# Norm sums by pairs, an earlier second batch, and four rest rows together in the head of a linear-attention and two-MLP kernel

## The chip, the cores and the metric

One core of one Trainium2 chip. The metric is the device time of one execution in microseconds. Before the change three runs took 1415.94, 1416.15 and 1416.86; the median is 1416.15.

## The reference

```python
kv  = einsum('bhsd,bhse->bhde', k, v)        # batch 8, heads 8, seq 576, head_dim 64
o   = einsum('bhsd,bhde->bhse', q, kv)
o   = o / sqrt(mean(o * o, axis=-1) + 1e-6) * g_norm
x   = o.transpose(0, 2, 1, 3).reshape(4608, 512)
h   = x @ w_in                               # 512 x 2048
x2  = (h * cos(h)) @ w_out                   # 2048 x 512
out = ((x2 @ w1) * (x2 @ w2)) @ w3 @ w_out2  # d_ff 1024
```

All arithmetic is float32 or finer; the weights arrive as 64-bit floats.

## The kernel before, in words

The order of every engine's instructions is written out by hand (`manual_schedule`): an engine runs its instructions in the order in which the Python code issues them, and waits at one whose operands are not there. So is the order of the DMA queue on SyncE (SP).

**Units, pairs, tiles.** A batch has two units (halves of 288 rows) and four pairs of heads. Units 0 and 1 are the first batch, 2 and 3 the second. The tokens are cut into tiles of 512 rows (TB); the products with `w_in` go in steps. Steps 0 to 7 are tile 0 with the eight first 128-column chunks of `w_in`, steps 8 to 15 tile 1 with the same chunks, and so on. A step is `emit_h`: twelve TensorE matmuls of 512 columns, because both `x` and `w_in` are held as a high and a low half (float32r) and three products of the halves are summed for each of four row blocks. In steps 0 to 8 the products that need the halves that come last stand last (L1065).

**What a step needs and leaves.** `w_in[m]` is made from chunk m: ScalarE and VectorE turn 64-bit words into float32 by five instructions (L157 on ScalarE, then L158, L159, L162, L167 on VectorE; `begin()` issues the first, `two()` the next two), and `put` splits the result: the high half on ScalarE (L123), the low half (L125) on VectorE for chunks 0 and 6 and on GpSimd for the others. Behind a step, ScalarE rounds (`rounded`, L654), VectorE reduces the angle (`reduced`, L657), ScalarE takes the sine (`sine`, L662) and VectorE multiplies by h (`gelu`, L666); this last one releases the step's bank. In the later loop (`phases`) the same four are L1942, L1943, L1912 and L1913.

**Norms.** For each pair and unit, ScalarE squares the outputs (`emit_square`) and keeps a scaled copy (`emit_keep`). `emit_sums` sums the squares over the head dimension on TensorE: 128 x 32 weights that pick a row, 96 columns at a time (T3), three matmuls for each unit. Their results land in 32 output partitions given by the pair (`place(p)`). Nine VectorE instructions (`norms`) take the inverse root of all at once. Then a spread brings each row back to 128 partitions: matmuls of 32 x 128 weights (`emit_row`, L502), one row group of 32 partitions for each pair, and VectorE multiplies the kept outputs by them (`emit_scale`, L519). `split_x` makes the high half of x (ScalarE, L1025) and the low half (VectorE or GpSimd, L1026).

A bank of PSUM holds 512 columns, but two units of a pair have 576. So the first spread covers 512 of them, and the remaining 64 are spread one pair at a time between the later steps (`rest_of`, one lone matmul). The second spread covers 480; the remaining 96 of unit 3 are done at the top of steps 8, 9, 10 and 11 (`left_row`), and their scaling in the middle of these (`left_scale`). All of these rests use the bank acc3, which step 6 also uses.

**Order around the change.** `first_batch` runs the first batch's kv sums, outputs, squares, sums, norms and spread, the second batch's kv sums, step 0, and the second batch's outputs of pair 0. `first_steps` runs steps 1 to 8 with the second batch in them: pair n's squares and sums in step n, its outputs a step earlier; then its norms, the spread and the low halves of tile 1. `phases` follows: at step n it issues step n + 1 on TensorE, the events of later batches (step 10's is the first, kv sums of the third batch, in the bank acc2 of step 8), and the four instructions of step n. Loads of the third batch's k and v wait in SP's queue for the buffers ("stage") in which the rounded values of steps 6 and 7 lie, its second pair of query loads for a buffer of the spread's weights.

Of the kernel before, what the change touches and what calls it, by code (L numbers as in the profile page):

```python
# [7 lines left out]
F32 = mybir.dt.float32  # L8
# [26 lines left out]
def kernel(  # L35
# [182 lines left out]
    def put_w_in(m):  # L218
        def put(f):
            t = wi_tile(m, f"w_in{m}")  # L220
            split(t.rearrange("p i k f -> p i (k f)"), f, nc.vector if m in (0, 6) else nc.gpsimd)
            w_in[m] = t
        return put

# [257 lines left out]
            o_sb[u] = ap.tile([P, NPAIR, HALF], F32, tag="osb", bufs=3, name=f"o_{u}")  # L482
        nc.scalar.activation(o_sb[u][:, p, :], o_ps.pop((u, p)), AF.Identity, scale=gneg)

    def place(p):
        return slice(32 * p, 32 * p + 32)

    def emit_sums(p, us, sums):
        for u in us:
            for k in range(NT3):  # L490
                i = 2 * (NT3 * (u % NHALF) + k)
                nc.tensor.matmul(
                    sums[place(p), 0:T3], picks["sums"][:, IN_ALL - i:IN_ALL - i + 32],
                    squares[u, p][:, T3 * k:T3 * k + T3], start=i == 0, stop=True,
                    skip_group_check=True,
                )
        for u in us:
            squares.pop((u, p))

    def emit_row(u, p, k, y, ps, c, start=True, part=slice(0, T3)):  # L500
        at = place(p)
# [5 lines left out]
    def emit_rows(us, width, banks, y):  # L507
        c = 0
        for u in us:
            for k in range(NT3):  # L510
                w = min(T3, width - c)
                for p in range(NPAIR):
                    if w > 0:
                        emit_row(u, p, k, y, banks[p], c, c == 0, slice(0, w))
                c += w

    def emit_scale(u, p, ps, c, s=slice(0, HALF)):
        o = o_sb[u][:, p, s]
        nc.vector.tensor_tensor(o, o, ps[:, c:c + s.stop - s.start], ALU.mult)  # L519

    def emit_scales(us, p, ps, width):
        emit_scale(us[0], p, ps, 0)
        emit_scale(us[1], p, ps, HALF, slice(0, width - HALF))

    def norms(sums, y):

# [4 lines left out]
    def first_batch(y, ones, g_row):  # L531

        sums = ps_h.tile([P, 512], F32, tag="h", name="ms_first")
        idle = ps_h.tile([P, 512], F32, tag="h", name="idle")
        units, seconds = range(NHALF), range(NHALF, 2 * NHALF)

        def begin():
            c = chunks[state["conv"]]
            state["conv"] += 1
            made = c.convert()  # L540
            next(made)
            return made
# [12 lines left out]
        emit_kv(0, 0, lambda: busy(2))  # L555
        copy_kv(0)
        g_ps = ps_a.tile([P, 512], F32, tag="pa", name="g_ps")
        nc.tensor.matmul(
            g_ps[:, 0:1], g_row, ones[:, 0:1],
            start=True, stop=True,  # L560
        )
        busy(2)
        for p in range(NPAIR):
            for u in units:
                emit_whole(u, p, ps_acc.tile(
                    [P, 512], F32, tag=f"acc{(2 * p + u) % 4}", name=f"out_{u}_{p}"
                )[:, 0:HALF])
            for u in units:
                emit_square(u, p)
            if p == 2:  # L570
                first = begin()
            if p + 1 < NPAIR:
                emit_kv(0, p + 1)
                copy_kv(p + 1)
            else:
                busy(4)
                rest_of(first)
                put(1)
            if p == 0:
                nc.scalar.activation(gneg, g_ps[:, 0:1], AF.Copy, scale=-1.0)  # L580
            emit_sums(p, units, sums)
            for u in units:
                emit_keep(u, p)
        list(norms(sums, y))
        emit_kv(1, 0)
        copy_kv(0)
        second = begin()
        rest_of(second, 2)
        busy(4)
        emit_kv(1, 1)  # L590
        copy_kv(1)
        banks = [
            ps_acc.tile([P, 512], F32, tag=f"acc{p}", name=f"spread1_{p}") for p in range(NPAIR)
        ]
        emit_rows(units, TB, banks, y)
        later = ps_h.tile([P, 512], F32, tag="h", name="kv_later0")
        emit_kv(1, 2, ps=later[:, 0:D])
        emit_kv(1, 3)
        for p in range(2):
            emit_scales(units, p, banks[p], TB)  # L600
            split_x(0, p, lows=nc.gpsimd)
        h = emit_h_parts(0)
        next(h)
        next(h)
        for p in range(2, NPAIR):
            emit_scales(units, p, banks[p], TB)
        for p in range(2, NPAIR):
            split_x(0, p)
        copy_kv(2)
        copy_kv(3)  # L610
        next(h)
        next(h)
        for v in seconds:
            out_bank(v, 0)
        next(h, None)
        third = begin()
        rest_of(second, 2)
        put(1)
        emit_h(1)
        rest_of(third, 2)  # L620
        return third

    def out_bank(v, p):
        emit_whole(v, p, two_banks(v, p, f"out_{v}_{p}")[:, 0:HALF])
# [6 lines left out]
    def first_steps(y_first, y, made):  # L631

        units = range(NHALF, 2 * NHALF)
        far = units[-1]
# [38 lines left out]
        def more():  # L673
            prefetch(min(state["put"] + 8, n_first))

        WIDE = HALF + 2 * T3
        cut = TB - HALF

        def rest_of(p):
            ps = ps_acc.tile([P, 512], F32, tag="acc3", name=f"spread1_rest{p}")  # L680
            emit_row(1, p, NT3 - 1, y_first, ps, 0, part=slice(cut - 2 * T3, T3))
            return ps

        more()
        for n in range(NPAIR):
            if n:
                gelu(n - 1)
                rest = rest_of(n - 1)
                emit_h(n + 1)
            rounded(n)  # L690
            reduced(n)
            if n:
                keep(n - 1)
            for v in units:
                emit_square(v, n)
            two(made)
            if n:
                emit_scale(1, n - 1, rest, 0, slice(cut, HALF))
            sine(n)
            new = begin()  # L700
            put(1)
            more()
            two(new)
            made = new
            emit_sums(n, units, sums)
            if n + 1 < NPAIR:
                for v in units:
                    out_bank(v, n + 1)
        n = NPAIR
        gelu(n - 1)  # L710
        rest = rest_of(n - 1)
        emit_h(n + 1)
        rounded(n)
        reduced(n)
        keep(n - 1)
        two(made)
        emit_scale(1, n - 1, rest, 0, slice(cut, HALF))
        sine(n)
        new = begin()
        norm = norms(sums, y)  # L720
        next(norm)
        put(1)
        more()
        emit_h(n + 2, "acc3")
        next(norm, None)
        spread = [
# [13 lines left out]
        split_x(1, slice(0, KD), (NHALF - 1,), nc.gpsimd)  # L740
        for p in range(NPAIR):
            emit_scales(units, p, spread[p], WIDE)
            if p < 2:
                split_x(1, p, units, nc.gpsimd)
        reduced(n + 1)
        split_x(1, 2, units)
        split_x(1, 3, units)
        emit_h(HM)
        sine(n + 1)
        gelu(n + 1)  # L750
# [2 lines left out]
        rounded(n + 3)  # L753
        new = begin()
        gelu(n + 2)
        reduced(n + 3)
        sine(n + 3)
        two(new)
        gelu(n + 3)
        two(new)  # L760
        spare.append(chunks[HM].tag)
        put(1)

        left = {}

        def left_row(p):
            left[p] = ps_acc.tile([P, 512], F32, tag="acc3", name=f"spread2_rest{p}")
            emit_row(far, p, NT3 - 1, y, left[p], 0)

        def left_scale(p):  # L770
            emit_scale(far, p, left.pop(p), 0, slice(2 * T3, HALF))

        for p in range(NPAIR):
            at(HM + p, "top", left_row, p)
            at(HM + p, "mid", left_scale, p)

    plan = {}

# [1211 lines left out]
    if True:  # L1990
# [45 lines left out]
        with tc.manual_schedule(  # L2036
# [4 lines left out]
        ):  # L2041
            load_first(g_row)
            made = first_batch(parts[2], ones, g_row)
            first_steps(parts[2], parts[3], made)
            x0 = phases()

            wstack.close()
# [90 lines left out]
```

## Time and profile before

| what | value |
|---|---|
| profiled execution, its own time | 1414.61 us |
| its span | 1412.8 us |
| median of the runs | 1416.15 us |
| TensorE (PE) busy | 1401.9 us, 99% |
| VectorE (DVE) busy | 968.0 us, 69% |
| ScalarE (ACT) busy | 717.4 us, 51% |
| GpSimd (POOL) busy | 577.5 us, 41% |
| chain that ended last, by engine | PE 90%, DVE 5%, DMA 2% |

The chain is followed back from the last instruction through whatever released each step. The share of an engine in the chain is not its busy time. PE instructions appear once for each of the two passes of a float32 matmul, so six small matmuls are twelve records; the products of float32r halves are one record each. Records overlap, as matmuls are pipelined: what a group takes is read from its start to the start of the next. A wait is shown in brackets behind the instruction that waited, with the engine, tensor and line that released it. The granted clock of TensorE (PEclk) is the share of full speed.

### The profile page before, as it was taken

The page shows a single profiled execution, that of the slowest core. Times are in us where ns is not written, and L with a number is a line of the kernel's source. Part 1 is how long each engine was busy: PE and PEld are TensorE (multiplying, and loading weights), DVE is VectorE, ACT ScalarE, POOL GpSimd, SP SyncE. Part 2 cuts the span into 40 slices and gives each one's busy share as a digit, 9 for nine tenths or more (in the row PEclk, how much of TensorE's full clock was granted, in tenths as well). Part 3 has the DMA queues.
Part 4 walks back from the last instruction along what each step waited for, and adds up shares of the span by engine and source line. Part 5 has one row for each costly group of instructions (what it writes and reads, how often), then busy time and mean ns, then how long its engine had stood idle before and what let it go on. Part 6 is the DMA issues. An engine that isn't in the chain of part 4 may idle for free.

```text
span 1412.8 us, 23304 instructions
## 1 busy us (share of the span) xinstructions
PE 1401.9 (99%) x8330; PEld 1233.7 (87%) x8330; DVE 968.0 (69%) x1545; ACT 717.4 (51%) x1335; POOL 577.5 (41%) x466
## 2 busy tenths in 40 slices
PE   9999999999999999999999999999999999999999
PEld 7677777777788888988888888999999999999999
DVE  4787475574779856788988857576654556855553
ACT  5665555545656655455555545443442333555553
POOL 3265663685386522232222429884760433200000
PEclk9999999999999999999999999999999999999999
DMA  9366986987798998999999982544444344786762
GB/s 350 118 230 203 331 247 216 303 278 258 234 322 312 331 336 294 321 350 340 337 336 372 362 299 109 178 152 140 140 145 140 96 145 140 241 282 216 255 216 109
DMA packets 209481, 345.55 MB, mean 245 GB/s; under 512 B 18933, under 2 KB 118613, under 8 KB 208981
## 3 DMA queue, kind: packets, MB, share of 16 engines
q1 hardware_dynamic: 209088, 343.77, 71.8%
q8 instruction: 65, 1.06, 0.3%
q14 instruction: 52, 0.42, 0.1%
q10 hardware_dynamic: 276, 0.30, 0.1%
HBM read 205.89 MB, written 138.11 MB: 243 GB/s over the span
## 4 chain that ended last, share of the span: by engine, by line
PE 90%; DVE 5%; DMA 2%; issue 1%; POOL 1%; ACT 1%; SPq 1%; ACTq 0%; DVEq 0%; POOLq 0%
PE X L1584 14%; PE X L1229 13%; PE h L1031 8%; PE h L1033 8%; PE h L1032 8%; PE oX L1687 7%; PE V L1584 7%; PE V L1229 6%; PE oV L1687 4%; PE Y L1229 3%; PE Y L1584 3%; PE oY L1687 2%; PE event L306 1%; PE event L802 1%; PE h L1065 1%
## 5 line engine op out<-in xcount | busy, mean ns | idle before, releaser
L1584 PE MATMUL X<-xc,w 128*128 128x384 f32 x1152 | 215.6, 334 | 0.0
L1031 PE MATMUL h<-x,w_in 128*128 128x512 f32 x540 | 214.9, 398 | 0.0
L1033 PE MATMUL h<-x,w_in 128*128 128x512 f32 x540 | 211.1, 391 | 0.0
L1032 PE MATMUL h<-x,w_in 128*128 128x512 f32 x540 | 211.1, 391 | 0.0
L1584 PEld LDWEIGHTS X<-xc,w 128*128 128x128 f32 x1152 | 201.0, 188 | 0.4 <-ACT s L1592 0.3
L1229 PE MATMUL X<-g_hl,wl 128*128 128x512 f32 (+1 forms) x960 | 199.7, 368 | 0.0
L1229 PEld LDWEIGHTS X<-g_hl,wl 128*128 128x128 f32 x960 | 167.3, 189 | 30.1 <-DVE wl L125 0.2
L125 POOL TENSOR_TENSOR g_hl<-g_raw,g_hl 128x1024 fp32r<-128x1024 f32 x29 | 73.3, 2529 | 233.4 <-ACT g_hl L123 187.0
L125 DVE TENSOR_TENSOR g_hl<-g_raw,g_hl 128x1024 fp32r<-128x1024 f32 x97 | 140.1, 1471 | 39.9 <-ACT g_hl L123 39.6
L123 ACT ACTIVATE g_hl<-g_raw 128x1024 fp32r<-128x1024 f32 x126 | 130.2, 1056 | 61.8 <-DMA g_raw<-g 57.5
L1942 ACT ACTIVATE r<-h 128x512 int32<-128x512 f32 x136 | 81.4, 598 | 153.3 <-PE h L1033 151.7
L1943 DVE SCALAR_TENSOR_TENSOR u<-h,r 128x512 f32<-128x512 f32 x128 | 88.0, 687 | 103.3 <-ACT r L1942 87.3
L1592 ACT ACTIVATE s<-X 128x384 f32<-128x384 f32 x144 | 70.7, 492 | 169.7 <-PE X L1584 169.7
L125 POOL TENSOR_TENSOR xc<-x2r,xc 128x768 fp32r<-128x768 f32 x49 | 94.9, 1964 | 104.4 <-ACT xc L123 104.2
L1031 PEld LDWEIGHTS h<-x,w_in 128*128 128x128 f32 x540 | 101.7, 188 | 32.9 <-issue 4.9
L1033 PEld LDWEIGHTS h<-x,w_in 128*128 128x128 f32 x540 | 101.8, 188 | 21.9
L1032 PEld LDWEIGHTS h<-x,w_in 128*128 128x128 f32 x540 | 101.7, 188 | 20.3
L1687 PE MATMUL oX<-wq,ab_hl 128*128 128x256 f32 x864 | 109.8, 283 | 0.0
L1584 PE MATMUL V<-xc,w 128*128 128x384 f32 x576 | 107.9, 334 | 0.4 <-DVE Y L1640 0.4
L1687 PEld LDWEIGHTS oX<-wq,ab_hl 128*128 128x128 f32 x864 | 106.5, 192 | 0.0
L1584 PEld LDWEIGHTS V<-xc,w 128*128 128x128 f32 x576 | 100.5, 188 | 0.7 <-DVE Y L1640 0.7
L1229 PE MATMUL V<-g_hl,wl 128*128 128x512 f32 (+1 forms) x480 | 100.6, 369 | 0.0
(220 smaller groups left out, 2442.4 us busy)
## 6 DMA issues: line engine op xcount, KB each, us to landing
g_raw<-g SPq DMA_DIRECT2D x126, 512.0 KB
ab_raw<-ab SPq DMA_DIRECT2D x34, 768.0 KB
ab<-q SPq DMA_DIRECT2D x96, 192.0 KB
kvraw<-in_kv_main_dram SPq DMA_DIRECT2D x32, 512.0 KB
g<-ta SPq DMA_DIRECT2D x32, 512.0 KB
g<-tb SPq DMA_DIRECT2D x32, 512.0 KB
ab<-s SPq DMA_DIRECT2D x72, 192.0 KB
g<-u SPq DMA_DIRECT2D x24, 512.0 KB
```

What stands on the lines that cost most here:

```text
L123: hi = nc.scalar.activation(dst[:, 0], src, AF.Copy)
L125: lo = lo_engine.tensor_tensor(dst[:, 1], src, f32(dst[:, 0]), ALU.subtract)
L306: nc.tensor.matmul(ps[D * j:D * (j + 1), d], keys[:, d], values[:, d], start=i == 0 and h == 0, stop=i == NC, skip_group_check=True,)
L1031: nc.tensor.matmul(ps, w[0], x[0], start=first, stop=False)
L1032: nc.tensor.matmul(ps, w[0], x[1], start=False, stop=False)
L1033: return nc.tensor.matmul(ps, w[1], x[0], start=False, stop=last).ins
L1229: nc.tensor.matmul(ps, w[:, a, i2, ws], g[:, b, q], start=first and half == 0 and q == 0 and n == 0, stop=last and final and q == KH - 1 a ...
L1584: nc.tensor.matmul(ps, w[:, self.i, a, k], x[:, b, k], start=first and k == 0 and n == 0, stop=last and k == 1 and n == 2, skip_group_chec ...
L1592: nc.scalar.activation(s, ps, AF.Copy)
L1687: nc.tensor.matmul(ps, t[:, a, k], w[:, b], start=first and k == 0 and n == 0, stop=last and k == 3 and n == 2, skip_group_check=True,)
L1942: nc.scalar.activation(r, h_ps[n], AF.Identity, bias=0.25, scale=INV_2PI)
L1943: nc.vector.scalar_tensor_tensor(u, h_ps[n], INV_2PI, r, ALU.mult, ALU.subtract)
```

## The change

- Chunk 5's low half goes from GpSimd to VectorE.
- First batch: the sums of the squares put (unit, pair) into its own group of 32 output columns (`spot`), so that the two units take turns matmul by matmul. The spread gives each unit and pair a bank of its own with all 288 columns: pairs 0 and 1 together, then pair 2, then pair 3 between two kv sums. The rests of the first batch no longer exist.
- Second batch: outputs and squares move a step or more forward (pairs 0 and 1 have their outputs before step 1). The sums come for two pairs at a time, taking turns (`sum_pairs`), before step 2 and before step 4.
- The second batch's four rests stand together behind step 8, in four banks, and their scaling together on VectorE.
- The low half of x for pair 1 of tile 1 goes from GpSimd to VectorE.

In the diff below short statements stand joined on one line.

```diff
-            split(..., nc.vector if m in (0, 6) else nc.gpsimd)
+            split(..., nc.vector if m in (0, 5, 6) else nc.gpsimd)
...
+    def spot(u, p):
+        first = 32 * (2 * (p % 2) + u % NHALF)
+        return slice(first, first + 32)
     def emit_sums(p, us, sums):
-        for u in us:
-            for k in range(NT3):
-                i = 2 * (NT3 * (u % NHALF) + k)
+        for k in range(NT3):
+            i = 2 * (NT3 * (p // 2) + k)
+            for u in us:
                 nc.tensor.matmul(
-                    sums[place(p), 0:T3], picks["sums"][:, IN_ALL - i:IN_ALL - i + 32],
-                    squares[u, p][:, T3 * k:T3 * k + T3], start=i == 0, stop=True,
+                    sums[spot(u, p), 0:T3], picks["sums"][:, IN_ALL - i:IN_ALL - i + 32],
+                    squares[u, p][:, T3 * k:T3 * k + T3], start=p < 2 and k == 0, stop=True,
...
+    def emit_spread(ps, us, banks, y):
+        for k in range(NT3):
+            for p in ps:
+                for u in us:
+                    at = spot(u, p)
+                    nc.tensor.matmul(
+                        banks[u, p][:, T3 * k:T3 * k + T3], picks[p // 2][at, k], y[at],
+                        start=k == 0, stop=True, skip_group_check=True)
...
+    def sum_pairs(ps, us, sums):
+        for u in us:
+            for k in range(NT3):
+                i = 2 * (NT3 * (u % NHALF) + k)
+                for p in ps:
+                    nc.tensor.matmul(sums[place(p), 0:T3], ..., squares[u, p][...], start=i == 0, ...)
...
     # first_batch, behind the norms
-        emit_rows(units, TB, banks, y)
+        emit_spread((0, 1), units, banks, y)      # banks acc0 to acc3
+        emit_spread((2,), units, banks, y)        # two banks "pa"
         emit_kv(1, 2, ps=later[:, 0:D])
-        emit_kv(1, 3)
-        for p in range(2):
-            emit_scales(units, p, banks[p], TB)
-            split_x(0, p, lows=nc.gpsimd)
+        scale(0); split_x(0, 0, lows=nc.gpsimd); scale(1); split_x(0, 1, lows=nc.gpsimd)
+        emit_spread((3,), units, banks, y)        # acc0, acc1 again
         h = emit_h_parts(0)
         next(h)
+        emit_kv(1, 3, ps=later[:, 0:D])           # acc2
         next(h)
-        for p in range(2, NPAIR): emit_scales(units, p, banks[p], TB)
+        scale(2); scale(3)
...
-        for v in seconds:
-            out_bank(v, 0)
+        for p in range(2):
+            for v in seconds:
+                out_bank(v, p)
         next(h, None)
         third = begin()
+        for v in seconds:
+            emit_square(v, 0)
...
     # first_steps: the loop over pairs is written out (square, outs are new short helpers)
+        rounded(0); square(1); reduced(0); two(made); sine(0); made = begin(); keep(0)
+        put(1); more(); two(made)
+        gelu(0); sum_pairs((0, 1), units, sums); outs(2); emit_h(2); rounded(1); reduced(1)
+        new = begin(); sine(1); keep(1); two(made); put(1); more(); square(2); two(new); made = new
+        gelu(1); outs(3); emit_h(3); rounded(2); reduced(2); new = begin(); square(3)
+        two(made); sine(2); put(1); more(); two(new); made = new
+        gelu(2); sum_pairs((2, 3), units, sums); emit_h(4); rounded(3); reduced(3)
+        new = begin(); keep(2); sine(3); two(made); gelu(3); put(1); more(); two(new); made = new
         n = NPAIR
-        gelu(n - 1); rest = rest_of(n - 1)
         emit_h(n + 1)
         rounded(n)
-        reduced(n); keep(n - 1); two(made); emit_scale(1, n - 1, rest, 0, ...); sine(n); new = begin()
+        keep(n - 1); new = begin(); two(made); reduced(n)
         norm = norms(sums, y)
         next(norm); put(1); more()
+        sine(n)
         emit_h(n + 2, "acc3")
         next(norm, None)
...
         for p in range(NPAIR):
             emit_scales(units, p, spread[p], WIDE)
-            if p < 2:
+            if p == 0:
                 split_x(1, p, units, nc.gpsimd)
         reduced(n + 1)
-        split_x(1, 2, units); split_x(1, 3, units)
+        for p in range(1, NPAIR):
+            split_x(1, p, units)
         emit_h(HM)
...
         gelu(n + 2)
+        left = [... banks acc0, acc1 for odd p, "pa" for even p ...]
+        for p in range(NPAIR):
+            emit_row(units[-1], p, NT3 - 1, y, left[p], 0)
         reduced(n + 3)
         sine(n + 3)
+        for p in range(NPAIR):
+            scale_part(units[-1], p, left[p], 0, slice(2 * T3, HALF))
...
-        for p in range(NPAIR):
-            at(HM + p, "top", left_row, p)
-            at(HM + p, "mid", left_scale, p)
```

## Rows read from the trace of the kernel before

**Rows 1.** Who TensorE waited for: total us, times, longest.
```profile
PE h L1065 <- ACT w_in L123: 1.7, 2, 1.1
...
PE event L306 <- DMA kvraw<-in_kv_main_dram: 0.8, 1, 0.8
```

**Rows 2.** TensorE in order of time: start, us, line, operands, records, idle before.
```profile
23.05 1.54 PE L502 MATMUL spread<-rs_first,pick 32*128 32x96 f32 x48
24.52 0.69 PE L284 MATMUL kv_later<-kvraw 128*64 128x64 f32 x16
...
25.40 0.69 PE L284 MATMUL kv<-kvraw 128*64 128x64 f32 x16
...
36.87 0.43 PE L502 MATMUL spread_rest<-rs_first,pick 32*128 32x64 f32 x2
37.23 3.02 PE L1065 MATMUL h<-x,w_in 128*128 128x512 f32 x12
40.17 1.18 PE L492 MATMUL ms_second<-sq,rs_first 128*32 128x96 f32 x12
41.28 1.24 PE L470 MATMUL out<-q,rs_first 128*128 128x288 f32 x4
...
68.46 0.46 PE L502 MATMUL spread_rest<-rs_first,pick 32*128 32x96 f32 x2 [2.08 <-DVE u_first L666]
68.84 0.52 PE L1031 MATMUL h<-x,w_in 128*128 128x512 f32 x1
...
73.81 0.46 PE L502 MATMUL spread_rest<-rs_first,pick 32*128 32x96 f32 x2 [0.37 <-DVE o L519]
...
80.50 1.15 PE L306 MATMUL event<-kvraw 128*64 128x64 f32 x32
```

**Rows 3.** Stretches: busy us (records) of PE, PEld, DVE, ACT, POOL, PEclk, DMA share, GB/s.
```profile
8.00:24.00 16.00, 16.00 (x212) 12.88 (x214) 5.97 (x16) 10.77 (x30) 0.00 (x0) 1.00 1.03 384
...
70.00:72.00 2.00, 2.00 (x6) 1.59 (x5) 1.69 (x3) 0.24 (x1) 0.00 (x0) 0.50 0.90 239
```

**Rows 4.** VectorE in order of time, the same columns as rows 2.
```profile
20.32 0.26 DVE L528 TENSOR_SCALAR rs_first<-ms_first 128x96 f32<-128x96 f32 x1 [0.29 <-PE ms_first L492]
...
46.55 0.69 DVE L657 SCALAR_TENSOR_TENSOR u_first<-h,r 128x512 f32<-128x512 f32 x1 [0.93 <-ACT r L654]
...
49.71 0.43 DVE L158 TENSOR_SCALAR i_f<-i_f 128x512 f32<-128x512 f32 x1 [1.00 <-ACT i_f L157]
...
52.13 0.69 DVE L657 SCALAR_TENSOR_TENSOR u_first<-h,r 128x512 f32<-128x512 f32 x1 [0.93 <-ACT r L654]
...
54.19 0.25 DVE L528 TENSOR_SCALAR rs_first<-ms_second 128x96 f32<-128x96 f32 x1
...
54.85 0.69 DVE L125 TENSOR_TENSOR w_in<-i_f,w_in 128x512 fp32r<-128x512 f32 x1 [0.16 <-ACT w_in L123]
...
60.23 2.60 DVE L519 TENSOR_TENSOR o<-o,spread 128x288 f32<-128x288 f32 x8
...
63.34 2.48 DVE L1026 TENSOR_TENSOR x<-o,x 128x288 fp32r<-128x288 f32 x4
65.75 0.67 DVE L666 TENSOR_TENSOR u_first<-u_first,h 128x512 f32<-128x512 f32 x1
...
72.91 0.69 DVE L1943 SCALAR_TENSOR_TENSOR u<-h,r 128x512 f32<-128x512 f32 x1 [1.18 <-ACT r L1942]
...
75.61 0.68 DVE L1913 TENSOR_TENSOR u<-u,h 128x512 f32<-128x512 f32 x1
76.20 0.24 DVE L519 TENSOR_TENSOR o<-o,spread_rest 128x96 f32<-128x96 f32 x1
```

**Rows 5.** Low halves of x: two by shape on VectorE, and GpSimd in order of time.
```profile
L1026 DVE TENSOR_TENSOR x<-o,x 128x160 fp32r<-128x160 f32 x1 | 0.9, 924 | 0.0
...
L1026 DVE TENSOR_TENSOR x<-o,x 128x160 fp32r<-128x160 f32 x1 | 0.3, 310 | 0.0
...
61.71 3.56 POOL L1026 TENSOR_TENSOR x<-o,x 128x256 fp32r<-128x256 f32 x5
```

More of the change, by code (lines that the diff above doesn't have):

```diff
@@ L220, in put @@
             t = wi_tile(m, f"w_in{m}")
-            split(t.rearrange("p i k f -> p i (k f)"), f, nc.vector if m in (0, 6) else nc.gpsimd)
+            split(t.rearrange("p i k f -> p i (k f)"), f, nc.vector if m in (0, 5, 6) else nc.gpsimd)
             w_in[m] = t
@@ L483, in emit_keep @@
         nc.scalar.activation(o_sb[u][:, p, :], o_ps.pop((u, p)), AF.Identity, scale=gneg)
-    def place(p):
-        return slice(32 * p, 32 * p + 32)
+    def spot(u, p):
+        first = 32 * (2 * (p % 2) + u % NHALF)
+        return slice(first, first + 32)
     def emit_sums(p, us, sums):
-        for u in us:
-            for k in range(NT3):
-                i = 2 * (NT3 * (u % NHALF) + k)
+        for k in range(NT3):
+            i = 2 * (NT3 * (p // 2) + k)
+            for u in us:
                 nc.tensor.matmul(
-                    sums[place(p), 0:T3], picks["sums"][:, IN_ALL - i:IN_ALL - i + 32],
-                    squares[u, p][:, T3 * k:T3 * k + T3], start=i == 0, stop=True,
+                    sums[spot(u, p), 0:T3], picks["sums"][:, IN_ALL - i:IN_ALL - i + 32],
+                    squares[u, p][:, T3 * k:T3 * k + T3], start=p < 2 and k == 0, stop=True,
                     skip_group_check=True,
@@ L498, in emit_sums, with emit_scale, place @@
             squares.pop((u, p))
+    def emit_spread(ps, us, banks, y):
[5 more added lines that the diff above has]
+                        banks[u, p][:, T3 * k:T3 * k + T3], picks[p // 2][at, k], y[at],
+                        start=k == 0, stop=True, skip_group_check=True,
+                    )
+    def emit_scale(u, p, ps):
+        o = o_sb[u][:, p, :]
+        nc.vector.tensor_tensor(o, o, ps[:, 0:HALF], ALU.mult)
+    def place(p):
+        return slice(32 * p, 32 * p + 32)
+    def sum_pairs(ps, us, sums):
[3 more added lines that the diff above has]
+                for p in ps:
+                    nc.tensor.matmul(
+                        sums[place(p), 0:T3], picks["sums"][:, IN_ALL - i:IN_ALL - i + 32],
+                        squares[u, p][:, T3 * k:T3 * k + T3], start=i == 0, stop=True,
+                        skip_group_check=True,
+                    )
+        for u in us:
+            for p in ps:
+                squares.pop((u, p))
     def emit_row(u, p, k, y, ps, c, start=True, part=slice(0, T3)):
@@ L515, in emit_rows, with scale_part @@
                 c += w
-    def emit_scale(u, p, ps, c, s=slice(0, HALF)):
+    def scale_part(u, p, ps, c, s=slice(0, HALF)):
         o = o_sb[u][:, p, s]
@@ L521, in emit_scales @@
     def emit_scales(us, p, ps, width):
-        emit_scale(us[0], p, ps, 0)
-        emit_scale(us[1], p, ps, HALF, slice(0, width - HALF))
+        scale_part(us[0], p, ps, 0)
+        scale_part(us[1], p, ps, HALF, slice(0, width - HALF))
     def norms(sums, y):
@@ L591, in first_batch, with room, scale @@
         copy_kv(1)
-        banks = [
-            ps_acc.tile([P, 512], F32, tag=f"acc{p}", name=f"spread1_{p}") for p in range(NPAIR)
-        ]
-        emit_rows(units, TB, banks, y)
+        banks = {}
+        def room(u, p):
+            if p == 2:
+                ps = ps_a.tile([P, 512], F32, tag="pa", name=f"spread_{u}_{p}")
+            else:
+                ps = ps_acc.tile(
+                    [P, 512], F32, tag=f"acc{(2 * (p % 3) + u) % 4}", name=f"spread_{u}_{p}"
+                )
+            banks[u, p] = ps
+        def scale(p):
+            for u in units:
+                emit_scale(u, p, banks[u, p])
+        for p in range(3):
+            for u in units:
+                room(u, p)
+        emit_spread((0, 1), units, banks, y)
+        emit_spread((2,), units, banks, y)
         later = ps_h.tile([P, 512], F32, tag="h", name="kv_later0")
         emit_kv(1, 2, ps=later[:, 0:D])
-        emit_kv(1, 3)
-        for p in range(2):
-            emit_scales(units, p, banks[p], TB)
-            split_x(0, p, lows=nc.gpsimd)
+        scale(0)
+        split_x(0, 0, lows=nc.gpsimd)
+        scale(1)
+        split_x(0, 1, lows=nc.gpsimd)
+        for u in units:
+            room(u, 3)
+        emit_spread((3,), units, banks, y)
         h = emit_h_parts(0)
         next(h)
+        later = ps_acc.tile([P, 512], F32, tag="acc2", name="kv_later1")
+        emit_kv(1, 3, ps=later[:, 0:D])
         next(h)
[L605 to L608, printed above, removed]
+        scale(2)
+        scale(3)
+        split_x(0, 2)
+        split_x(0, 3)
         copy_kv(2)
@@ L629, in two_banks, with first_steps @@
         return ps_acc.tile([P, 512], F32, tag=f"acc{v % NHALF}", name=name)
-    def first_steps(y_first, y, made):
+    def first_steps(y, made):
         units = range(NHALF, 2 * NHALF)
-        far = units[-1]
         sums = ps_acc.tile([P, 512], F32, tag="acc2", name="ms_second")
@@ L674, in more, with square @@
             prefetch(min(state["put"] + 8, n_first))
[L676 to L693, printed above, removed]
+        def square(n):
@@ L694, in first_steps, with outs @@
             for v in units:
                 emit_square(v, n)
[L696 to L708, printed above, removed]
+        def outs(n):
+            for v in units:
+                out_bank(v, n)
@@ new lines, in first_steps @@
+        WIDE = HALF + 2 * T3
+        more()
+        rounded(0)
+        square(1)
+        reduced(0)
+        two(made)
+        sine(0)
+        made = begin()
+        keep(0)
+        put(1)
+        more()
+        two(made)
+        gelu(0)
+        sum_pairs((0, 1), units, sums)
+        outs(2)
+        emit_h(2)
+        rounded(1)
+        reduced(1)
+        new = begin()
+        sine(1)
+        keep(1)
+        two(made)
+        put(1)
+        more()
+        square(2)
+        two(new)
@@ new lines, in first_steps @@
+        made = new
+        gelu(1)
+        outs(3)
+        emit_h(3)
+        rounded(2)
+        reduced(2)
+        new = begin()
+        square(3)
+        two(made)
+        sine(2)
+        put(1)
+        more()
+        two(new)
+        made = new
+        gelu(2)
+        sum_pairs((2, 3), units, sums)
+        emit_h(4)
+        rounded(3)
+        reduced(3)
+        new = begin()
+        keep(2)
+        sine(3)
+        two(made)
+        gelu(3)
+        put(1)
+        more()
@@ L709, in first_steps @@
+        two(new)
+        made = new
         n = NPAIR
-        gelu(n - 1)
-        rest = rest_of(n - 1)
         emit_h(n + 1)
         rounded(n)
+        keep(n - 1)
+        new = begin()
+        two(made)
         reduced(n)
[L715 to L719, printed above, removed]
         norm = norms(sums, y)
@@ L742, in first_steps @@
             emit_scales(units, p, spread[p], WIDE)
-            if p < 2:
+            if p == 0:
                 split_x(1, p, units, nc.gpsimd)
         reduced(n + 1)
-        split_x(1, 2, units)
-        split_x(1, 3, units)
+        for p in range(1, NPAIR):
+            split_x(1, p, units)
         emit_h(HM)
@@ L755, in first_steps @@
         gelu(n + 2)
+        left = [
+            ps_acc.tile([P, 512], F32, tag=f"acc{p // 2}", name=f"spread2_rest{p}") if p % 2
+            else ps_a.tile([P, 512], F32, tag="pa", name=f"spread2_rest{p}")
+            for p in range(NPAIR)
+        ]
+        for p in range(NPAIR):
+            emit_row(units[-1], p, NT3 - 1, y, left[p], 0)
         reduced(n + 3)
         sine(n + 3)
+        for p in range(NPAIR):
+            scale_part(units[-1], p, left[p], 0, slice(2 * T3, HALF))
         two(new)
@@ L762, in first_steps @@
         put(1)
[L764 to L771, printed above, removed]
-        for p in range(NPAIR):
-            at(HM + p, "top", left_row, p)
-            at(HM + p, "mid", left_scale, p)
     plan = {}
@@ L2043 @@
             made = first_batch(parts[2], ones, g_row)
-            first_steps(parts[2], parts[3], made)
+            first_steps(parts[3], made)
             x0 = phases()
```

## Prediction

> **What bounds the kernel now.** I read the page's shares first, then the waits and the order of time of each engine over the first 110 us, where everything that changes runs. TensorE is busy for 99% of the span. After the head its longest wait is 0.8 us, for a load [rows 1], so a microsecond by which it passes that point sooner is a microsecond of the end. The head is different. On TensorE the reader is to see two kinds of time to win. First, small matmuls that run one behind the other: the six of one pair's sums take 1.11 us, 0.185 each, and a lone row of a spread 0.36 to 0.38 [rows 2]. Second, idle time: at 66.4 us TensorE stops for 2.08 us, because the first rest of the second batch's norms takes the bank of step 6, which VectorE frees only then [rows 2]. Behind it the granted clock is 0.50, the lower of the two levels [rows 3], and step 9 takes 4.60 us (68.84 to 73.81, less 0.37 of waiting) instead of the 2.94 of a step at full clock: 1.66 us more [rows 2]. Two waits for weights add 1.7 us, the longer one 1.1 [rows 1].
>
> From 52 to 73 us the chain runs on VectorE, which is hardly idle there [rows 4]. So the change is worth what VectorE allows, up to the point where TensorE's slack against it is used up. I therefore follow both engines; "earlier" is against the time before.
>
> **First batch, to its norms.** The sums of the two units now write two groups of 32 columns in turn. No row shows two such groups of 96 elements. Bounds: 0.061 us a matmul, as 24 rows spread over four row groups take (1.47 us) [rows 2], and 0.185, no overlap. The nearest row is step 10's kv sums, two column groups in turn, 16 matmuls of 64 elements within 1.15 us, 0.072 each [rows 2]; for 96 elements that is 0.108, and I take 0.11. Six cost 0.65 instead of 1.11: 0.46 saved in each of four pairs, 1.84. But the norms stood only 0.29 us behind VectorE's own work [rows 4], the low half of chunk 0. That hangs on ScalarE, whose squares and copies move up by about 1.1, so VectorE is ready at 20.03 - 1.1 = 18.95 instead of 20.32: **1.4 earlier**. Nine instructions of 0.26 with their gaps (2.55) end at 21.5.
>
> **First spread to step 3.** TensorE from 21.5: the spread of two pairs in four row groups, 12 x 0.061 = 0.74; the third and fourth pair in two row groups, 6 x 0.10 = 0.6 each (0.061 and 0.185 are the bounds again); two kv sums of 0.88 [rows 2]; step 0's twelve matmuls 2.94; two pairs of outputs instead of one, 2 x 1.17. Together 8.98, to 30.5. VectorE hides its part: its scales start at 22.4, and the eight, four of them now 288 instead of 224 wide, with four low halves end by 27.5, before the 29.5 at which step 0's last matmuls want them. The fourth pair's banks need the first pair's scales (23.1), the outputs' banks the fourth's (25.3); TensorE arrives later at both. The 1.1 us wait for step 1's weights goes. Then step 1 2.94, the sums of two pairs in two column groups 12 x 0.11 = 1.3, outputs 1.17, step 2 2.94, outputs 1.17, step 3 2.94: 12.46, to 42.95. No rest rows stand between (four of 0.36 before). Step 3 ended at 45.75 (step 2 at 40.17, and steps stood 5.58 apart [rows 2, 4]): **2.8 earlier**. ScalarE's high halves for steps 2 to 4 come 1.4 to 2 us ahead of need by the same replay.
>
> **VectorE, step 3 to step 8.** From the reduction of step 3 (46.55) to the second norms (54.19) VectorE took 7.64 us, with 1.00 and 0.93 of waiting [rows 4]. The waits go, since it is now behind; so do two small scales (0.35); chunk 5's low half comes over from GpSimd, 0.60 (from 54.85 to the next instruction) [rows 4]. 7.64 - 1.93 - 0.35 + 0.60 = 5.96, so the norms start at 49.7, **4.5 earlier**. TensorE has steps 4 to 6 meanwhile and the spread by 54.5. It then waits some 1.5 us for the product of step 4 and the weights of step 7; neither existed as an idle of that size here before.
>
> Norms, chunk 7 and the eight scales are unchanged. Before the lows stood four halves at 2.41 us (63.34 to 65.75) [rows 4]; now six, as pair 1 comes over from GpSimd. Beside a busy GpSimd one of 160 elements took 0.924, alone 0.310 [rows 5]; 288 elements alone follow at 0.36. GpSimd was at its lows from 61.71 for 3.56 us [rows 5]; without pair 1 it is done 2.2 us after their start, at 59.4 in the new time. VectorE's lows start at 58.8. So one pair of blocked size (1.0) and two free pairs (0.59 each): 2.2, the same within 0.2: **4.7 earlier** at 65.75. Then the four rests' scales stand in one go ahead of step 7's product, four of 0.24 or less [rows 4], 0.7 with their overlap: 4.0 earlier at step 8's reduction (72.91). The one that stood behind that reduction is gone (0.17): 4.2 earlier at step 8's product, which ended at 76.3 and now at 72.1.
>
> **TensorE, step 7 to step 12.** Step 7 starts at 56.0, steps 7 and 8 end at 61.9, the four rests in four row groups cost 0.45 instead of 4 x 0.38, and they take banks of the spread that were freed by 58.7, so the 2.08 us wait and the half clock go. Steps 9 to 11 follow, to 71.1; step 10 takes a rest's bank, whose scale comes at 64.3, before the 65.2 of need. The kv sums of step 10 take step 8's bank and wait for its product: 72.2 against 80.50 [rows 2], **8.3 earlier**. The batch's loads on SP's queue stand behind the reductions of steps 6 and 7, which come 4.5 us sooner; the query loads no longer stand behind a rest. The rest of pair 3 that followed is gone, 0.4: **8.7 us**. From there VectorE's backlog, 4 us sooner, meets TensorE with 0.3 us to spare at step 13 and more later.
>
> The profiled execution took 1414.61 (span 1412.8 and 1.8 around it), 1.5 below the median of the runs, 1416.15. It would be 1405.9; for the median I say **1407.4**.
>
> **Rivals.**
> 1. VectorE is blocked by GpSimd. If GpSimd still works when all six lows run, each costs what three of the four cost before, 0.72 (2.41 less 0.25 for the free one, by three): 4.3 instead of 2.2, the gain is 6.6, the time 1409.5. For it: both engines move up. Against: GpSimd has one pair fewer. The Trainium skill says it as a rule ("SBUF — State Buffer", Who interferes with whom): a VectorE instruction with two SBUF inputs contends with a GpSimd instruction that reads SBUF. The trace agrees, 0.924 against 0.310 [rows 5]. Chance 0.15.
> 2. The clock falls in a new idle gap. It fell behind 2.08 us, and did not behind 1.1. The new gaps are 1.5 and 1.1. Behind the first, 1.66 is mostly absorbed by the second (0.6 left); behind the second all of it counts: 1408.0 to 1409.1. Chance 0.15.
> 3. Two groups do not overlap: the norms keep their time (1.4), the first two pairs' sums take 2.2 (0.9), the two spreads 1.1 each (1.0): gain 5.4, 1410.8. Chance 0.10.
> 4. Slower: changing the column or row group from one matmul to the next costs what a lone row costs, 0.36 from 36.87 to 37.23 [rows 2]. First sums 24 x 0.36 = 8.6 instead of 4.4, so the norms come 4.2 later and not 1.4 earlier; the two spreads 4.3 instead of 1.2; the first sums of pairs 4.3 instead of 1.3. That takes 11.7 from 8.7: 1419.2. It decides from about 0.29 a matmul (0.11 + 8.7/48). Against it: step 10's kv sums, which change group each time at 0.072. The Trainium skill ("TensorEngine Tiling (Array Packing)", Key Properties) says that a change of tiling mode drains the engine, while tiles of one mode run in parallel; the lone row, between two modes, and the kv sums agree. Chance 0.04.
> 5. The change does not do what it says for the first batch: its loads set the pace. The DMA share was 1.03 from 8 to 24 us [rows 3], though TensorE hardly waited for a load. The first 1.4 is lost: 1408.8. Chance 0.06.
>
> **Numbers.** The forecast has 0.50. Below it lies full overlap in two groups (0.061): 0.5 for the spreads, 0.6 for the sums of pairs, 1406.3, and free lows, down to 1405.3. Above lie rivals 1 to 3, to 1411.5. A measurement of this kernel can tell 0.2%, 2.8 us, from no change. Rivals 1, 2, 3 and 5 are each faster by more; only two or three together come within 2.8. So faster 0.88, same 0.07, slower 0.05.
>
> **What would show it.** Right: sums of pairs about 1.3 us; the second norms near 49.7; step 7 near 56; four rests within half a microsecond near 62; step 10's kv sums near 72 with a wait for step 8's product; clock 1.00 throughout. Wrong: a granted clock under 1 behind 54 or 72 us, six lows of 4 us, sums of pairs over 2 us, or an idle TensorE between 73 and 95 us, which would mean that VectorE's backlog holds longer than to step 10.

## The result and the profile after

The changed kernel took 1403.9 us (median of six; 1402.5 to 1404.7) beside 1415.7 for the kernel before (six runs, the three named at the start among them): ratio 0.9918, 95% interval 0.9905 to 0.9932. One of the changed kernel's six runs took 1913.25 us at a granted clock of 0.67 and counts in the median alone, not in the range and the ratio. In a later set of five it took 1404.35, ratio 0.9929 (0.9916 to 0.9941). It is faster, as forecast, by more than forecast: 1407.4 was said, and 1403.9 lies 1.4 us below the range. The profiled execution took 1403.8, its span 1402.0 (1412.8 before).

TensorE in order of time, the same columns as [rows 2]; the lines answer to the first outputs, the first spread, the sums, the outputs with a step behind them, the rests, and step 10's kv sums:
```profile
8.00 1.17 PE L470 MATMUL out<-q,rs_first 128*128 128x288 f32 x4
...
21.87 1.58 PE L506 MATMUL spread<-rs_first,pick 32*128 32x96 f32 x36 [0.34 <-DVE rs_first L377]
...
33.80 1.18 PE L523 MATMUL ms_second<-sq,rs_first 128*32 128x96 f32 x24
34.92 1.24 PE L470 MATMUL out<-q,rs_first 128*128 128x288 f32 x4
35.78 3.12 PE L1146 MATMUL h<-x,w_in 128*128 128x512 f32 x12
38.74 1.13 PE L470 MATMUL out<-q,rs_first 128*128 128x288 f32 x4
...
42.57 1.19 PE L523 MATMUL ms_second<-sq,rs_first 128*32 128x96 f32 x24
...
55.56 5.75 PE L1146 MATMUL h<-x,w_in 128*128 128x512 f32 x24 [1.47 <-ACT w_in L123]
61.24 0.48 PE L534 MATMUL spread_rest<-rs_first,pick 32*128 32x96 f32 x8
61.64 0.50 PE L1112 MATMUL h<-x,w_in 128*128 128x512 f32 x1
...
71.60 1.15 PE L306 MATMUL event<-kvraw 128*64 128x64 f32 x32 [1.48 <-DVE u L1994]
72.58 0.40 PE L306 MATMUL event<-kvrest 128*64 128x64 f32 x8
72.91 0.50 PE L1112 MATMUL h<-x,w_in 128*128 128x512 f32 x1
```
The four rests take 0.40 us and wait for nothing; the 2.08 us wait of [rows 2] is gone, and two shorter ones, 1.47 and 1.48, have come where the prediction put them (1.5 and 1.1). VectorE, the same columns as [rows 4]:
```profile
19.18 0.25 DVE L560 TENSOR_SCALAR rs_first<-ms_first 128x96 f32<-128x96 f32 x1
...
43.37 0.69 DVE L712 SCALAR_TENSOR_TENSOR u_first<-h,r 128x512 f32<-128x512 f32 x1 [0.33 <-ACT r L709]
...
49.55 0.24 DVE L560 TENSOR_SCALAR rs_first<-ms_second 128x96 f32<-128x96 f32 x1
...
55.33 2.60 DVE L551 TENSOR_TENSOR o<-o,spread 128x288 f32<-128x288 f32 x8
...
58.45 2.13 DVE L1107 TENSOR_TENSOR x<-o,x 128x288 fp32r<-128x288 f32 x6
60.51 0.68 DVE L721 TENSOR_TENSOR u_first<-u_first,h 128x512 f32<-128x512 f32 x1
...
68.33 0.69 DVE L2024 SCALAR_TENSOR_TENSOR u<-h,r 128x512 f32<-128x512 f32 x1 [1.19 <-ACT r L2023]
...
70.87 0.68 DVE L1994 TENSOR_TENSOR u<-u,h 128x512 f32<-128x512 f32 x1
```
From 43 to 68 us its longest waits are 0.70 and 1.19 us, both for ScalarE: it sets the head, and six low halves cost 2.06 us (58.45 to 60.51) where four had cost 2.41. Stage by stage, in us earlier than before:

| place | before | forecast | after | measured |
|---|---|---|---|---|
| first norms | 20.32 | 1.4 | 19.18 | 1.1 |
| step 3's end on TensorE | 45.75 | 2.8 | 42.57 | 3.2 |
| second norms | 54.19 | 4.5 | 49.55 | 4.6 |
| step 5's product | 65.75 | 4.7 | 60.51 | 5.2 |
| step 8's reduction | 72.91 | 4.0 | 68.33 | 4.6 |
| step 10's kv sums | 80.50 | 8.3 | 71.60 | 8.9 |
| step 12 | 82.20 | 8.7 | 72.91 | 9.3 |
| end of the span | 1412.8 | 8.7 | 1402.0 | 10.8 |

Three places of the kernel before that the table and the explanation need, besides the rows ahead of the prediction: its first outputs, outputs with a step right behind them, and step 12.
```profile
7.69 1.14 PE L470 MATMUL out<-q,rs_first 128*128 128x288 f32 x4
...
28.46 1.13 PE L470 MATMUL out<-q,rs_first 128*128 128x288 f32 x4
29.22 1.30 PE L1045 MATMUL h<-x,w_in 128*128 128x512 f32 x4
...
82.20 0.50 PE L1031 MATMUL h<-x,w_in 128*128 128x512 f32 x1
```
TensorE reached its first outputs at 8.00 us with the change and at 7.69 before, and nothing of the change stands ahead of them. Counted from there, the first norms come 1.45 us sooner (forecast 1.4) and step 12 comes 9.6 sooner (forecast 8.7).

### The profile page after: what moved, and what is told of

Same layout as the page of the kernel before. It is cut to its first block, busy times and chain, and to the rows that moved or that the text cites. A ratio compares the mean times of both kernels' runs of the same rounds, so it can differ in the third digit from the quotient of the medians.

```text
span 1402.0 us, 23282 instructions
## 1 busy us (share of the span) xinstructions
PE 1393.3 (99%) x8322; PEld 1229.1 (88%) x8322; DVE 966.7 (69%) x1544; ACT 717.3 (51%) x1335; POOL 575.9 (41%) x463
## 4 chain that ended last, share of the span: by engine, by line
PE 94%; DVE 3%; DMA 2%; issue 1%; ACT 0%; SPq 0%; DVEq 0%; ACTq 0%
PE X L1310 14%; PE X L1665 14%; PE h L1112 9%; PE h L1113 8%; PE h L1114 8%; PE oX L1768 7%; PE V L1310 7%; PE V L1665 7%; PE oV L1768 4%; PE Y L1310 4%; PE Y L1665 3%; PE oY L1768 2%; PE event L306 1%; PE event L883 1%; DMA w3raw<-w 1%
## 5 line engine op out<-in xcount | busy, mean ns | idle before, releaser
L125 DVE TENSOR_TENSOR g_hl<-g_raw,g_hl 128x1024 fp32r<-128x1024 f32 x97 | 136.4, 1433 | 44.0 <-ACT g_hl L123 43.7
```

## The experiments

**The rests put back.**
```diff
-        left = [... four banks ...]
-        for p in range(NPAIR):
-            emit_row(units[-1], p, NT3 - 1, y, left[p], 0)
...
-        for p in range(NPAIR):
-            scale_part(units[-1], p, left[p], 0, slice(2 * T3, HALF))
...
+        for p in range(NPAIR):
+            at(HM + p, "top", left_row, p)     # bank acc3
+            at(HM + p, "mid", left_scale, p)
```


> The changed kernel with one part undone: the second batch's four rests stand again at the tops of steps 8 to 11, all in step 6's bank, their scaling in the middle of these steps. Theory (VectorE's product of step 6 and then each rest's scaling gate TensorE): the first rest waits about 1.9 us for step 6's product (63.2 us), the second and third wait for the scaling before them, step 10's kv sums start near 74.8 instead of 71.60 and step 12 near 76.5 instead of 72.91, so the end is 3.6 us later, about 1407.5. Rival (the rests cost only their own matmuls, 4 x 0.38 less 0.45): 1.1 us later, about 1405. If the clock falls again behind the first rest, step 9 takes 4.6 us, but most of that is covered by the wait for the scaling.

TensorE in order of time, then a stretch of it (columns as in [rows 3]):
```profile
63.22 0.46 PE L534 MATMUL spread_rest<-rs_first,pick 32*128 32x96 f32 x2 [1.96 <-DVE u_first L721]
68.57 0.46 PE L534 MATMUL spread_rest<-rs_first,pick 32*128 32x96 f32 x2 [0.36 <-DVE o L551]
71.91 0.46 PE L534 MATMUL spread_rest<-rs_first,pick 32*128 32x96 f32 x2
75.26 1.15 PE L306 MATMUL event<-kvraw 128*64 128x64 f32 x32
```
```profile
66.00:68.00 2.00, 2.00 (x6) 1.40 (x5) 0.82 (x2) 1.48 (x3) 0.77 (x1) 0.56 1.03 308
```
The wait of 1.96 and the half clock are back. Step 12 starts at 76.97, 4.06 later than with the change (theory 3.6, rival 1.1). The median is 1409.0, ratio to before 0.9959 (0.9946 to 0.9971); it lies 4.7 to 5.1 above the two medians of the changed kernel.

**The rests alone**, put into the kernel before by the mirror of that diff.

> The kernel before with one part of the change alone: the four rests at once behind step 8, in four banks, scaled together. Theory (TensorE then waits for VectorE's product of step 8): rests near 66.4 us without a wait, clock 1.00, step 10's kv sums ready at 75.3 but started near 76.9, when step 8's product is done, so 3.6 us sooner than 80.50, and 4.0 us at step 12 and at the end: about 1411.7. Rival (all that the idle time, the half clock and the lone rows cost comes back): 2.08 + 1.66 + 0.37 + 1.1 = 5.2 us, about 1410.5.

```profile
76.90 1.15 PE L306 MATMUL event<-kvraw 128*64 128x64 f32 x32 [1.61 <-DVE u L1909]
```
To the place as the theory had it, 76.9. Step 12 starts at 78.2 and the clock stays at 1.00. By this landmark (the start of step 12) the rests are worth 4.0 us in either direction, so of 9.3 the other edits bring 5.3. How these 5.3 divide is known in part only: no run undoes the earlier second batch or the first spread's new banks by themselves. The median, 1409.65, ratio 0.9964 (0.9950 to 0.9978), lies nearer the rival's 5.2; its interval holds both. The landmark decides for the theory: 3.6 sooner at step 10.

**No turns.** The same matmuls, one column group after the other.
```diff
-        for k in range(NT3):
-            for u in us:
+        for u in us:
+            for k in range(NT3):
...
-        for u in us: for k in range(NT3): for p in ps:
+        for p in ps: for u in us: for k in range(NT3):
```


> The changed kernel with the same matmuls in another order: all sums of one unit and pair stand together, so that no two neighbours change the group of output columns. Theory (neighbours in two groups overlap, 0.10 us a matmul against 0.185): first batch's sums 1.11 us instead of 0.63 for a pair, first norms 1.4 us later (20.6 instead of 19.18), the sums of two pairs 2.2 instead of 1.12, step 3 ends 2.5 us later, step 10's kv sums near 74.1 instead of 71.60, the end 2.5 us later: about 1406.4. Rival (VectorE alone sets the head, TensorE's savings are hidden): under 0.5 us at step 10 and at the end.

```profile
34.04 1.87 PE L523 MATMUL ms_second<-sq,rs_first 128*32 128x96 f32 x24
...
72.55 1.15 PE L306 MATMUL event<-kvraw 128*64 128x64 f32 x32 [1.51 <-DVE u L1994]
```
Both were off. Twelve sums took 1.80 us instead of 1.12, so turns do overlap; but the first batch's six took 0.81, not 1.11, so that of the 1.84 us saved on its sums only 0.72 was taken back. Its norms started at 19.42 (19.18), right behind chunk 0's low half on VectorE, as with the change; counted from the first outputs, which came at 7.87, that is 0.36 later. Step 10 came 0.95 later, of which 0.24 was there at the first norms; the theory had said 2.5. The median is 1406.2, ratio 0.9938 (0.9926 to 0.9951). So the turns are worth about 0.7 us through the second batch, and 0.2 to 0.4 through the first.

**Both kernels once more.**

> The kernel before once more, for a second profile. From the start of step 12 to the span's end the profile of before took 1330.6 us and that of the changed kernel 1329.1, so 1.5 us of the gain arose after the head: 0.4 at a load of k and v at 220 us, 0.6 at a wait for VectorE at 692 us, 0.5 in small steps. Theory (these are chance of the one execution): the stretch comes out anywhere between 1329 and 1331, with other waits. Rival (the sooner head also shortens them): again 1330.6 within 0.3, with 0.8 us and 0.4 us of waiting at the same two places.

> The changed kernel once more, for a second profile and more times. Profiles so far took, from the start of step 12 to the span's end, 1330.6, 1330.1 and 1330.4 us with the early steps of the kernel before and 1329.1, 1329.3 and 1329.8 with those of the changed one. Theory (chance of the execution: waits of 0.1 to 1.0 us at two or three places that differ from run to run): between 1328.8 and 1330.6, step 12 near 72.9. Rival (the sooner head shortens the rest by about 1 us): 1329.1 within 0.3.

First outputs and step 12, of before and then with the change:
```profile
7.21 1.17 PE L470 MATMUL out<-q,rs_first 128*128 128x288 f32 x4
...
81.73 0.50 PE L1031 MATMUL h<-x,w_in 128*128 128x512 f32 x1
```
```profile
7.36 1.17 PE L470 MATMUL out<-q,rs_first 128*128 128x288 f32 x4
...
72.29 0.50 PE L1112 MATMUL h<-x,w_in 128*128 128x512 f32 x1
```
Step 12 is 9.4 us sooner, and counted from the first outputs 9.6, as in the first pair. From step 12 to the span's end the two took 1330.1 and 1330.1, where the first profiles had 1330.6 and 1329.1. The median of the set of before was 1414.8. What TensorE waited for in that stretch, with the change, first and second execution of the kernel:
```profile
PE V L1665 <- DVE Y L1721: 0.4, 1, 0.4
PE event L306 <- DMA kvraw<-in_kv_main_dram: 0.3, 1, 0.3
```
```profile
PE event L306 <- DMA kvraw<-in_kv_main_dram: 1.1, 1, 1.1
PE V L1665 <- DVE Y L1721: 0.4, 1, 0.4
```
The same load cost 0.8 before [rows 1], 0.3 in the second execution of before, 0.3 and 1.1 here. The waits move from execution to execution, in kernels of either head. Over all profiles the stretch took 1330.1 to 1330.6 with the early steps of before (three) and 1329.1 to 1330.9 with those of the change (eight, without the one with another bank). The rival is out in the size that it named; a smaller effect is not.

**Chunk 5 back on GpSimd** (`m in (0, 6)`).

> The changed kernel with chunk 5's low half back on GpSimd alone. Theory (VectorE's chain from step 3 to step 8 counts every instruction): second norms 0.6 us sooner (48.95 instead of 49.55), step 7 near 55.0, step 10's kv sums near 71.0 instead of 71.60. Rival (the move to VectorE paid, since step 5 would wait for GpSimd's slower low half): step 5 waits, or VectorE's next instructions are slowed by GpSimd, and step 10 is not sooner.

VectorE and GpSimd in order of time, then TensorE and a stretch, all of this kernel:
```profile
45.83 1.40 DVE L159 TENSOR_SCALAR i_f<-i_f 128x512 int32<-128x512 int32 x1
```
```profile
45.60 1.34 POOL L125 TENSOR_TENSOR w_in<-i_f,w_in 128x512 fp32r<-128x512 f32 x1 [2.46 <-ACT w_in L123]
```
```profile
55.21 7.31 PE L1146 MATMUL h<-x,w_in 128*128 128x512 f32 x24 [1.50 <-ACT w_in L123]
62.45 0.48 PE L534 MATMUL spread_rest<-rs_first,pick 32*128 32x96 f32 x8
71.26 1.15 PE L306 MATMUL event<-kvraw 128*64 128x64 f32 x32
```
```profile
57.00:59.00 2.00, 2.00 (x6) 1.51 (x6) 2.00 (x6) 1.65 (x5) 1.44 (x3) 0.52 0.71 242
```
The rival holds. VectorE's conversion, 0.43 us elsewhere, took 1.40 beside GpSimd's low half: 0.97 lost for 0.60 saved, and with it a wait of 0.18 for the high half. From the reduction of step 3 to the second norms it is 6.36 us against 6.18 (6.35 in the next kernel but one, which has the same edit). The prediction charged chunk 5's move 0.60 and gave it nothing back. The profile also shows what rival 2 had asked for: behind the gap of 1.50 the clock fell to 0.52, and steps 7 and 8 took 1.6 us more. TensorE then had no wait at step 10, so it cost next to nothing. This kernel, the next one and the one with another bank were executed once each: their landmarks are compared, not their times.

**Pair 1 back on GpSimd** (`if p < 2`).

> The changed kernel with the low halves of pair 1 of tile 1 back on GpSimd, so VectorE has four instead of six. Theory (VectorE with two operands from SBUF is held up while GpSimd works, so fewer but blocked): four take 2.2 to 2.4 us beside GpSimd against 2.06 for six, step 5's product 0.2 to 0.4 us later than 60.51, step 10's kv sums near 71.9. Rival (no hold-up, each at its free size): four take 1.2 us, step 5's product 0.85 sooner, step 10's kv sums near 70.8.

By shape, the columns as in [rows 5], with pair 1 on GpSimd and then with the change:
```profile
L1107 DVE TENSOR_TENSOR x<-o,x 128x288 fp32r<-128x288 f32 x2 | 1.4, 720 | 0.0
L1107 DVE TENSOR_TENSOR x<-o,x 128x160 fp32r<-128x160 f32 x2 | 1.2, 618 | 0.0
```
```profile
L1107 DVE TENSOR_TENSOR x<-o,x 128x288 fp32r<-128x288 f32 x3 | 1.6, 529 | 0.0
L1107 DVE TENSOR_TENSOR x<-o,x 128x160 fp32r<-128x160 f32 x3 | 0.9, 312 | 0.0
```
Four blocked halves cost 2.37 us to the next instruction, six mostly free ones 2.06. Step 10 came 28.54 us behind the reduction of step 3 instead of 28.23: 0.3 later, as the theory had it. Here too the clock fell, to 0.50 from 57 to 59 us, behind the gap of 1.50 at 55 us.

**Step 8's rounding first, and chunk 5 on GpSimd.** Chunk 8's split moves behind step 8's rounding and reduction.
```diff
         spare.append(chunks[HM].tag)
-        put(1)
+        at(HM, "mid", put, 1)
```


> The changed kernel with two edits: chunk 8's split is issued behind step 8's rounding and reduction instead of ahead of them, and chunk 5's low half is back on GpSimd. Theory (VectorE's path to step 8's product sets step 10): the rounding no longer waits in ScalarE's queue behind the split, so VectorE does not wait 1.19 us for it, and the 0.6 us of the low half goes: step 10's kv sums at 69.8 instead of 71.60 (TensorE is ready at 69.5), step 12 near 71.1, the end 1.8 us sooner. Rival (TensorE or the loads set step 10): at most 0.3 us.

```profile
68.83 0.70 DVE L158 TENSOR_SCALAR i_ps<-i_ps 128x512 f32<-128x512 f32 x1 [0.61 <-ACT i_ps L157]
```
Only 0.4 of the 1.8 was won (27.82 from step 3's reduction to step 10, 28.23 with the change). The 1.19 us wait is gone, but the split now stood ahead of chunk 9's first conversion on ScalarE, and VectorE waited 0.61 for that; chunk 5 lost its 0.18. The median is 1404.4.

**The split behind both**, chunk 5 left on VectorE.
```diff
-        put(1)
...
             plan_w_in(k, (8, 9, 10, 12, 14, 16, 18)[k - i])
+        at(HM, "mid", put, 1)
```


> The changed kernel with one edit: chunk 8's split stands behind step 8's rounding and reduction and behind the first conversion of chunk 9. Counted from the reduction of step 3, step 10's kv sums started 28.23 us later in both profiles of the changed kernel. Theory (VectorE's path to step 8's product sets step 10): VectorE no longer waits 1.19 us for the rounding of step 8, nor 0.61 us for chunk 9's conversion as it did when the split stood between, so 27.0 us, with about 0.3 us of waiting left on TensorE, step 12 and the end 1.2 us sooner, 1402.9. That is less than 0.2%, so the times will hardly tell it. Rival (something else gates step 10): 28.2.

```profile
70.50 1.15 PE L306 MATMUL event<-kvraw 128*64 128x64 f32 x32 [0.24 <-DVE u L1994]
```
From step 3's reduction (43.55) it is 26.95 us, as the theory said. Step 12 starts at 71.8. The median, 1403.3, ratio to before 0.9921 (0.9907 to 0.9935), is the lowest of all sets, but the times can't tell it from the changed kernel.

**Another bank for step 10.**
```diff
-            ps_acc.tile(..., tag=f"acc{2 + j}", ...)
+            ps_acc.tile(..., tag=f"acc{2 + j + (n == 10)}", ...)
```


> The changed kernel with step 10's kv sums in the bank acc3, which is free since step 6's product, instead of acc2, which waits for step 8's. Theory (VectorE's backlog is the bound, the bank only the place where it shows): no wait at step 10 (1.48 before), step 12 1.5 us sooner, but step 13 now waits about 1.1 us for step 9's product, so from step 14 on only 0.3 to 0.4 us are kept. Rival (the bank alone was late): the whole 1.5 us is kept to the end.

```profile
69.95 1.15 PE L306 MATMUL event<-kvraw 128*64 128x64 f32 x32
...
75.41 0.50 PE L1112 MATMUL h<-x,w_in 128*128 128x512 f32 x1 [1.13 <-DVE u L1994]
...
78.39 1.15 PE L306 MATMUL event<-kvraw 128*64 128x64 f32 x32
```
The wait of 1.48 is not removed but moved: step 13 waits 1.13 for step 9's product, and step 12's kv sums start 0.2 sooner than with the change (78.58; the theory said 0.3 to 0.4, the rival 1.5). The theory holds.

## Why the prediction came out as it did

**Right.** The mechanism and its order: VectorE sets the head from step 3 to step 8; the 2.08 us wait and the half clock go; step 10 waits for step 8's product. The rests alone land on 76.9 as worked out for that run, and the four rests put back cost their waits (4.06), not only their matmuls (1.1). Two column groups overlap (rivals 3 and 4 are out, 0.093 to 0.105 us a matmul against the 0.11 taken); GpSimd does not block the six lows (rival 1), and four of them it does. The clock stayed at 1.00 (rival 2), if narrowly, since it fell in two variants behind the same gap. The loads did not set the pace of the first batch (rival 5).

**Right, though the table hides it: the first batch's share.** Its sums were saved as forecast (0.63 instead of 1.11), chunk 0's low half moved up with ScalarE, and the norms no longer wait for TensorE. From the first outputs to the norms it is 1.45 us less than before in both pairs of profiles, where 1.4 was forecast. The 1.1 of the table is this less the 0.31 by which the first outputs came later in that execution.

**Mis-sized: TensorE's work from the first norms to step 3.** From the spread to step 3's end the prediction counted 21.45 us; it took 20.70. It summed outputs at 1.17 and a step at 2.94, 4.11 together, as they stood before a lone rest. Without the rest behind them, outputs and step took 3.82 (34.92 to 38.74). Each first rest had cost 0.29 beside its own 0.36; the trace of before had a row for it, outputs of 0.76 (28.46 to 29.22) where a step followed. Another 0.2 came from the sums of pairs, 1.12 instead of 1.3: the 0.11 was scaled from the kv sums' busy time of 1.15, and from start to start (0.98, 71.60 to 72.58) it would have been 0.092. With the 0.31 of the first outputs against it, step 3 ended 0.4 sooner than forecast. VectorE's own pieces added 0.2: 8.9 instead of 8.3 at step 10, 9.3 instead of 8.7 at step 12.

**The sum.** Forecast and median differ by 3.5. The head gives 0.9 (9.6 instead of 8.7), less 0.3 for the first outputs: 0.6 at step 12. Another 1.5 arose behind it (10.8 at the end for 9.3 there), and 1.4 came in because the profiled execution of before lay 1.5 under its median, which the forecast added, while that of after lies 0.1 under.

**Where it was wrong: the range.** With the head's error alone the forecast would have been 1406.8, inside the range. The step that failed is the last one, from step 12 to the median: "a microsecond by which it passes that point is a microsecond of the end", taken as exact, and with it the 1.5 us from the profiled execution to the median, taken over unchanged. In the profiled pair 9.3 at step 12 became 10.8 at the end, by waits that were 0.4 and 0.6 shorter at 220 and 692 us and 0.5 in small drifts. The second pair gave 9.4 and 9.4. The waits change from execution to execution, from 0.3 to 1.1 at one load alone. The profiled execution lay 1.5 and 1.2 under the median before, and 0.1 under it with the change both times; what makes this difference is not shown. The low end counted bounds of the head (0.061 us a matmul, free lows) and nothing for this spread, nor for that of the base: three runs had the median 1416.15, with three more it was 1415.7, and the later sets had 1413.8 to 1415.0. Both errors went the same way here; whether that was chance is not shown. The shift of the medians (11.8 and 10.6) is more than the 9.6 of the head, a ratio of 0.9932, which is the upper end of the first interval (0.9905 to 0.9932) and lies inside the second (0.9916 to 0.9941). Whether a microsecond beyond the head is real stays open.

## What to carry to other kernels

Where one engine is saturated and another sets the order in front of it, work out when the two meet again, and count from a point ahead of the change: so counted, that landmark was 9.6 us sooner in both pairs here, while the end (10.8 and 9.4) carries the spread of every later wait. Give the range room for that spread and for the base's own. An instruction is charged with what it blocks as well as with its time: a low half on the idle engine cost the busy one more than it took off it. A lone small matmul between large ones cost nearly twice its row in the trace here (0.65 for 0.36).

## What the runs showed of the hardware

- The granted clock was at half, the lower of its two levels, behind TensorE waits of 2.08 us [rows 2, 3], 2.09 (the kernel before once more) and 1.96 (the rests put back), and also behind 1.50 in two profiles (chunk 5 and pair 1 on GpSimd). Behind the gap of 1.3 to 1.5 at that place seven other profiles show 1.00, the changed kernel's, with its second gap of 1.48, among them. So a wait of 1.5 went either way here; each fall cost some 1.6 us of TensorE.
- VectorE's conversion with one operand from SBUF (a tensor_scalar, 128x512 int32, 0.43 us) took 1.40 beside a GpSimd instruction; one with two such operands had taken 0.924 for 0.310 [rows 5]. The Trainium skill ("SBUF — State Buffer", Who interferes with whom) names tensor_scalar too, among the instructions that can take the port pair shared with GpSimd. This row agrees; the prediction weighed the rule for two inputs alone.
- Matmuls of two column groups overlap even where the program has three of one group and then three of the other (0.81 for six, against 0.63 in turns and 1.11 in one group).
